# The low parts of eleven weight tiles are subtracted on GpSimd where VectorE did it

## The chip, the cores and the metric

The kernel runs on one core of one Trainium2 chip. The metric is the device time of one execution in microseconds (us); of several runs the median is given. The profile comes from one further execution. Engines are named as in the profile: PE is TensorE, DVE is VectorE, ACT is ScalarE, POOL is GpSimd, SP is the queue that starts DMAs.

## The reference

Attention with rotary positions (4 batches, 8 heads, 576 positions, head size 64) feeds a channel layer with a gate, and that a mixer of tokens and channels. Cut to what is computed:

```
attn = softmax(scale * rotate(q) @ rotate(k).T) @ v         # B=4, H=8, S=576, D=64
x    = attn, heads side by side                             # B x 576 x 512
xk, xr = mu * x + (1 - mu) * x_prev                         # mu_k and mu_r
v    = relu(xk @ w_k)**2 @ w_v                              # 512 -> 1024 -> 512
x    = sigmoid(xr @ w_r) * v                                # the gate: w_r is 512 x 512
h    = relu(x.T @ w_tok1) @ w_tok2                          # the token layer: 576 -> 256 -> 576
u    = x + h.T
out  = u + relu(u @ w_ch1) @ w_ch2                          # the channel layer: 512 -> 1536 -> 512
```

The weights arrive as 64-bit floats. Every product is made of two parts of each operand: `x` is rounded to a high part, and `x - high` is its low part; a product is then high*high + high*low + low*high.

## The kernel before, in words

**Stages.** Attention runs from the start to about 400 us. The channel layer of the middle (called K in the program) works through eight chunks (four batches, two halves of 288 positions), partly beside attention and from 400 us alone. Then come the gate and the token layer, from 488 us, and the last channel layer, from 597 us.

**One K chunk** (`kvr_gen`, L763). Eight groups of 12 products make `kp` (L751 to L753). Of each group ACT makes `t` (relu, L821) and the high part of its square `k2` (L825, called k in the profile); POOL makes the square again as `q` (L827); DVE subtracts, which gives the low part of `k2` (L828 through the helper `tt`, L111). The second product, `vp`, takes all eight `k2`, four groups of 24 products. For one `k2`, L751 and L753 need the high part, and L752 the low part. There are two buffers of `t`, two of `q`, and eight of `k2`.

**Weights** (class `Conv`, L183). Each weight tile passes four stages, in steps that take two tiles a time: SP loads its words (L207); ACT makes a first copy `cv` (L215); DVE turns the 64-bit words into 32-bit floats in `cv` with three instructions (L222, L226, L228), of which the second and third read `words` and `cv`; ACT writes the high part into `parts` (L80), and an engine subtracts, which gives the low part:

```
elif j == 3:
    dst, f = weights.take(k), self.t.pop(i).bitcast(F32)
    copy("A", dst[:, 0], f)
    tt(self.low, dst[:, 1], f, dst[:, 0].bitcast(F32), ALU.subtract)
```

The parameter `low` names that engine: "P" is POOL, anything else DVE. There are three `cv` buffers, so the ACT copy of the third tile on waits until the low part of a tile is subtracted. `conv0`, beside the start of attention, prepares the tiles of K, with "P". `conv1` (L995) prepares the four tiles of `w_r` (512 columns), five of `w_tok1` (256), two of `w_tok2` (576), and two of the last layer, which go another way (L246). It runs beside the last two K chunks, 433 to 475 us: the driver loop (L1050 to L1060) makes a step of `conv1` after every 45 products' worth of K.

**What sets the order.** The program names operations with priorities; a scheduler with a timing model of its own then fixes each engine's instruction order when the kernel is built. On the chip every engine takes its instructions strictly in that order, and waits on semaphores for what other engines owe it.

Of the kernel before, what the change touches and what calls it, by code (L numbers as in the profile page):

```python
# [16 lines left out]
B, H, S, D = 4, 8, 576, 64  # L17
# [14 lines left out]
HELD, LATE, EARLY = 5, 2, 2  # L32
# [39 lines left out]
def body(tc, kin, qin, vw, tabs, ident, mu, w_k, w_v, w_r, w_t1, w_t2, w_c1, w_c2, out):  # L72
# [41 lines left out]
    with ctx:  # L114
# [11 lines left out]
        P = {}  # L126
# [36 lines left out]
        def w3(w):  # L163
            return w.rearrange("(k p) f -> p k f", p=128)
# [516 lines left out]
        after = {}  # L681
# [191 lines left out]
        for j in range(2):  # L873
            for k in range(2):
# [3 lines left out]
        cv = Conv(lambda: P["xs"].tile([128, 2 * HS], I32, tag="xs", name="cv"),  # L878
                  wk + wv, "conv0", "rope", "P", lambda: acc_p.tile([128, 512], I32, tag="acc", name="cvp"))
# [32 lines left out]
        kv = Stream(kvr_gen([("K", b, c) for b in range(B) for c in range(2)], ready))  # L912
# [61 lines left out]
        def top(nm, bufs, st=mw):  # L974
            return st.enter_context(tc.tile_pool(name=nm, bufs=bufs, side="right"))

        cv_p = top("cv", 3)
        wr = Weights(top("wr", 1), [w3(w_r)[:, k] for k in range(KD)], [128, 2, DM])
        t1 = Weights(top("t1", 1), [w_t1[:, t] for t in range(5)], [128, 2, DTOK])
        t2 = Weights(top("t2", 1), [w_t2[:, m] for m in range(2)], [128, 2, S])  # L980
# [4 lines left out]
        def c2_part(a, b):  # L985
            w = Weights(top(f"c2{a}", 1), [w3(w_c2)[:, k] for k in range(a, b)], [128, 2, DM], raw_p, (rows2, a))
            c2_at.update({k: (w, k - a) for k in range(a, b)})
            return w
# [3 lines left out]
        def cv_t():  # L992
            return cv_p.tile([128, S], I32, tag="cv", name="cv")

        cv = Conv(cv_t, [wr, t1, t2, c2_part(0, EARLY)], "conv1", low="D", after="kv", then="out")  # L995
        def gate_gen(b):

            y = y_p[b].tile([128, KD, S], F32, tag="y", name="y")
# [73 lines left out]
        cv, cv3 = Conv(cv_t, [c1_w[0], c2_part(EARLY, HALF)], "conv2", low="D", after="gate"), Conv(cv_t, [c1_w[1], c2_b], "conv3", low="D", after="hs")  # L1072
# [234 lines left out]
```

## Time and profile before

| | |
|---|---|
| median of three runs | 901.6 us (901.35 to 908.77) |
| the profiled execution | 902.66 us, its span 900.8 us |
| mean granted PE clock | 0.988 of full |
| busy: PE, DVE, ACT, POOL | 839.5, 634.8, 515.3, 475.6 us |

The profile page gives sums over the span. The change touches only the stretch in which `conv1` runs, so the rows below come mostly from the timeline (instructions of one engine in order of time) and from the table of busy times by stretch, for 430 to 490 us. On the timeline a duration runs from an instruction's start to its end, and instructions of one engine overlap a little; how long each one holds its engine up is read from one start to the next.

### The profile page before, as it was taken

The numbers are of one execution on the slowest core, as the hardware profiler recorded it, in microseconds if no ns is written. First come the engines' busy times: TensorE is split into PE (matmuls) and PEld (weight loads), VectorE is DVE, ScalarE is ACT, GpSimd is POOL, SyncE is SP. The second block draws the span as 40 slices with busy tenths as digits, with TensorE's granted clock in tenths as the row PEclk, the third lists the DMA queues.
The fourth block names the chain that finished last, engine by engine and source line by source line (L and its number), as shares of the span: only waits on it lengthen the run. The fifth ranks groups of instructions, "written<-read, shape, count | busy, mean of one in ns | idle before, by whom it ended". The sixth has DMA issues, their size and how long they took to land.

```text
span 900.8 us, 18846 instructions
## 1 busy us (share of the span) xinstructions
PE 839.5 (93%) x7027; PEld 723.7 (80%) x7027; DVE 634.8 (70%) x1468; ACT 515.3 (57%) x1155; POOL 475.6 (53%) x506
## 2 busy tenths in 40 slices
PE   8899869898888899999999999999999999999998
PEld 5788757786776778799999989988878888888876
DVE  5889888887798788841793699956798355446332
ACT  4799678777777778863565656444556322223221
POOL 5999978988697666356344754311222222222221
PEclk9999979999999999999999999999999999999999
DMA  8786399999999979899332231201230000001000
GB/s 238 259 296 211 102 198 180 203 214 183 204 203 187 193 135 161 155 174 372 120 115 79 89 129 47 77 1 38 76 114 5 1 23 32 27 28 53 2 27 27
DMA packets 168651, 112.07 MB, mean 124 GB/s; under 512 B 132720, under 2 KB 148208, under 8 KB 168048
## 3 DMA queue, kind: packets, MB, share of 16 engines
q1 hardware_dynamic: 168560, 110.87, 49.6%
q8 instruction: 55, 0.90, 0.4%
q14 instruction: 36, 0.29, 0.1%
HBM read 60.90 MB, written 14.16 MB: 83 GB/s over the span
## 4 chain that ended last, share of the span: by engine, by line
PE 56%; DVE 17%; POOL 7%; ACT 7%; issue 6%; DMA 6%; SPq 1%; DVEq 0%; ACTq 0%; POOLq 0%
PE co L751 5%; PE c1p L751 5%; PE c1p L752 5%; PE c1p L753 5%; PE co L752 5%; PE co L753 5%; PE S L459 4%; DVE p L518 3%; PE pv L623 2%; DVE nm L477 2%; PE vp L751 2%; PE kp L751 2%; PE vp L752 2%; PE vp L753 2%; POOL rk L111 2%
## 5 line engine op out<-in xcount | busy, mean ns | idle before, releaser
L111 POOL TENSOR_TENSOR hs<-ht,hs 128x288 f16<-128x288 f32 x96 | 73.3, 764 | 229.6 <-DVE ht L1186 115.5
L1182 ACT ACTIVATE hs<-c1p,top 128x288 f16<-128x288 f32 x96 | 47.7, 497 | 161.7 <-PE c1p L753 161.7
L477 DVE TENSOR_REDUCE nm<-S 128x1 f32<-128x576 f32 x144 | 104.2, 748 | 16.1 <-PE S L459 15.1
L752 PE MATMUL c1p<-uhl,parts 128*128 128x288 f16 x384 | 109.8, 286 | 0.0
L753 PE MATMUL c1p<-uhl,parts 128*128 128x288 f16 x384 | 109.8, 286 | 0.0
L751 PE MATMUL c1p<-uhl,parts 128*128 128x288 f16 x384 | 109.6, 286 | 0.0
L752 PE MATMUL co<-hs,parts 128*128 128x288 f16 x384 | 108.7, 286 | 0.0
L753 PE MATMUL co<-hs,parts 128*128 128x288 f16 x384 | 108.7, 286 | 0.0
L751 PE MATMUL co<-hs,parts 128*128 128x288 f16 x384 | 105.1, 286 | 0.3 <-ACT hs L1182 0.3
L751 PEld LDWEIGHTS <-parts 128*128 128x128 f16 x768 | 75.0, 98 | 19.3 <-issue 0.5
L459 PE MATMUL S<-kq 64*128 64x288 f32 (+1 forms) x696 | 75.2, 317 | 16.2 <-ACT es L493 6.0
L751 PE MATMUL kp<-xs,parts 128*128 128x288 f32 x256 | 80.1, 316 | 11.0 <-ACT t L821 9.5
L752 PEld LDWEIGHTS <-parts 128*128 128x128 f16 x768 | 75.1, 98 | 18.8
L753 PEld LDWEIGHTS <-parts 128*128 128x128 f16 x768 | 75.2, 98 | 18.6
L1186 DVE TENSOR_SCALAR ht<-c1p,top 128x288 f32<-128x288 f32 x60 | 30.9, 515 | 77.6 <-ACT hs L1182 76.5
L111 POOL TENSOR_TENSOR q<-t 128x288 f32<-128x288 f32 x64 | 53.2, 835 | 59.2 <-ACT t L821 55.1
L459 PEld LDWEIGHTS S<-kq 64*128 64x128 f32 (+1 forms) x696 | 58.9, 191 | 30.2 <-ACT es L493 11.6
L751 PE MATMUL vp<-k,parts 128*128 128x288 f32 x256 | 77.2, 306 | 3.1 <-ACT vt L846 2.2
L518 DVE SCALAR_TENSOR_TENSOR p<-es,rc,p 128x576 f16<-128x576 f32 x60 | 68.0, 1137 | 13.8 <-ACT p L82 13.8
L752 PE MATMUL vp<-k,parts 128*128 128x288 f32 x256 | 76.7, 302 | 0.9 <-DVE k L111 0.9
L752 PE MATMUL kp<-xs,parts 128*128 128x288 f32 x256 | 76.6, 300 | 0.0
L753 PE MATMUL kp<-xs,parts 128*128 128x288 f32 x256 | 76.2, 298 | 0.0
(162 smaller groups left out, 2466.7 us busy)
## 6 DMA issues: line engine op xcount, KB each, us to landing
rq<-in_qin_dram SPq DMA_DIRECT2D x30, 320.0 KB, 4.0
rk<-in_kin_dram SPq DMA_DIRECT2D x30, 288.0 KB, 3.8
words<-in_w_c_dram SPq DMA_DIRECT2D x12, 512.0 KB, 3.8
words<-in_w_c_dram SPq DMA_DIRECT2D x16, 384.0 KB, 3.2
vr<-in_vw_dram SPq DMA_DIRECT2D x16, 320.0 KB, 3.4
xd<-xT SPq DMA_DIRECT2D x16, 288.5 KB, 2.8
xT<-xd SPq DMA_DIRECT2D x4, 1154.0 KB, 6.6
vd<-vt SPq DMA_DIRECT2D x32, 144.0 KB, 2.1
```

The source lines that it names most:

```text
L111: return (pool if e == "P" else dve).tensor_tensor(o, a, b, op=op)
L459: o = pe.matmul(S_t[j][:, h, 0:HS], lhsT=a[l, 128 * m:128 * m + 128], rhs=b[l, h * HS:(h + 1) * HS], start=(n == 0), stop=(n == 2))
L477: last["max"] = dve.tensor_reduce(out=nm, in_=S_t[j][:, :, 0:HS], op=ALU.max, axis=AX.XY, negate=True)
L518: o = last["lo"] = dve.scalar_tensor_tensor(out=t[:, 1], in0=e_t.pop(j), scalar=sum_t[j], in1=t[:, 0], op0=ALU.mult, op1=ALU.subtract)
L623: pe.matmul(p[l, 0:n], lhsT=v[:, a, l], rhs=ts[x][:, c, :], start=(i == 0), stop=(i == len(prods) - 1))
L751: pe.matmul(p, lhsT=wh, rhs=t[:, 0], start=first, stop=False)
L752: pe.matmul(p, lhsT=wh, rhs=t[:, 1], start=False, stop=False)
L753: pe.matmul(p, lhsT=wl, rhs=t[:, 0], start=False, stop=last)
L1182: last["hs"] = act.activation(out=h[:, 0], in_=p[:, 0:HS], func=AF.Relu, scale=g)
L1186: dve.tensor_scalar(out=f, in0=p[:, 0:HS], scalar1=g, scalar2=0.0, op0=ALU.mult, op1=ALU.max)
```

## The change

`conv1` gets "P" where it had "D":

```diff
-        cv = Conv(cv_t, [wr, t1, t2, c2_part(0, EARLY)], "conv1", low="D", after="kv", then="out")
+        cv = Conv(cv_t, [wr, t1, t2, c2_part(0, EARLY)], "conv1", low="P", after="kv", then="out")
```

Eleven subtractions go from DVE to POOL: four of 512 columns, five of 256, two of 576. The two tiles of the last layer go through L246 on DVE, as before. The scheduler makes its orders anew; they differ from before only in the stretch of the last two K chunks.

POOL's order in the chunk of batch 3, first half (`q` and `parts` with their numbers: `q_7085` is the square of the fourth `k2`, `q_7185` of the last; `parts_7207` is the last tile of `w_r`, `parts_7210` the first of `w_tok1`). Three subtractions of 512 columns stand further ahead in the same way.

```order
 L111 TENSOR_TENSOR q_7085<-t_7078 128x288
+L111 TENSOR_TENSOR parts_7207<-cv_7026,parts_7207 128x512
 L111 TENSOR_TENSOR q_7105<-t_7098 128x288
+L111 TENSOR_TENSOR parts_7210<-cv_7028,parts_7210 128x256
 L111 TENSOR_TENSOR q_7145<-t_7138 128x288
+L111 TENSOR_TENSOR parts_7294<-cv_7123,parts_7294 128x256
 L111 TENSOR_TENSOR q_7165<-t_7158 128x288
+L84 TENSOR_SCALAR a_7287<-xT_5620,om_s_74 128x288
+L111 TENSOR_TENSOR parts_7297<-cv_7125,parts_7297 128x256
 L111 TENSOR_TENSOR q_7185<-t_7178 128x288
-L84 TENSOR_SCALAR a_7287<-xT_5620,om_s_74 128x288
 L84 TENSOR_SCALAR a_7342<-xT_5620,om_s_74 128x288
```

Ahead of the last square, `q_7185`, POOL now has seven subtractions: four of 512 columns and three of 256.

DVE's order around the last `k2` of that chunk (`k2_7183`), before:

```order
L222 TENSOR_SCALAR cv_7125<-cv_7125 128x256
L738 SCALAR_TENSOR_TENSOR f_7254<-xT_5620,mu_s_73,a_7252 128x288
L111 TENSOR_TENSOR parts_7210<-cv_7028,parts_7210 128x256
L111 TENSOR_TENSOR k2_7183<-q_7185,k2_7183 128x288
L111 TENSOR_TENSOR parts_7294<-cv_7123,parts_7294 128x256
L226 SCALAR_TENSOR_TENSOR cv_7125<-words_7032,cv_7125 128x256
L111 TENSOR_TENSOR xs_7256<-f_7254,xs_7256 128x288
L222 TENSOR_SCALAR cv_7219<-cv_7219 128x256
```

The same place with the change:

```order
L111 TENSOR_TENSOR k2_7163<-q_7165,k2_7163 128x288
L111 TENSOR_TENSOR xs_7256<-f_7254,xs_7256 128x288
L226 SCALAR_TENSOR_TENSOR cv_7219<-words_7127,cv_7219 128x256
L222 TENSOR_SCALAR cv_7221<-cv_7221 128x256
L738 SCALAR_TENSOR_TENSOR f_7289<-xT_5620,mu_s_73,a_7287 128x288
L228 SCALAR_TENSOR_TENSOR cv_7219<-words_7127,cv_7219 128x256
L226 SCALAR_TENSOR_TENSOR cv_7221<-words_7129,cv_7221 128x256
L111 TENSOR_TENSOR k2_7183<-q_7185,k2_7183 128x288
L111 TENSOR_TENSOR xs_7291<-f_7289,xs_7291 128x288
```

Five subtractions ahead of `k2_7183` are gone from DVE (four of 512 columns, one of 256). In their place nine instructions that stood behind it now stand ahead of it: L226 and L228 of `cv_7125`; L222, L226 and L228 of `cv_7219`; L222 and L226 of `cv_7221`; one `xs`; one `f`.

PE's order where it first needs the low part of that `k2` (L752), before:

```order
L751 MATMUL vp_7233<-k2_7163,parts_1744 128x288
L752 MATMUL vp_7233<-k2_7163,parts_1744 128x288
L753 MATMUL vp_7233<-k2_7163,parts_1744 128x288
L752 MATMUL vp_7174<-k2_7183,parts_1747 128x288
L753 MATMUL vp_7174<-k2_7183,parts_1747 128x288
L751 MATMUL vp_7233<-k2_7183,parts_1747 128x288
```

With the change:

```order
L752 MATMUL vp_7268<-k2_7143,parts_1737 128x288
L753 MATMUL vp_7268<-k2_7143,parts_1737 128x288
L752 MATMUL vp_7174<-k2_7183,parts_1747 128x288
L753 MATMUL vp_7174<-k2_7183,parts_1747 128x288
L752 MATMUL vp_7233<-k2_7183,parts_1747 128x288
L753 MATMUL vp_7233<-k2_7183,parts_1747 128x288
L751 MATMUL vp_7268<-k2_7163,parts_1744 128x288
```

The first use of that low part stands 19 products later in PE's order, behind products of a third `vp` group. PE has the same number of products. On SP one load of `xT` (L1001) stands two stores earlier.

## Rows read from the trace of the kernel before

**Rows 1.** The page's first part: busy us, share of the span, instructions.

```profile
PE 839.5 (93%) x7027; PEld 723.7 (80%) x7027; DVE 634.8 (70%) x1468; ACT 515.3 (57%) x1155; POOL 475.6 (53%) x506
```

**Rows 2.** Table by stretch: us; busy PE, PEld, DVE, ACT, POOL; granted clock; DMA.

```profile
438.00:454.00 16.00, 15.85 (x120) 15.62 (x120) 16.00 (x31) 11.11 (x29) 7.46 (x9) 1.00 0.15 48
454.00:469.00 15.00, 15.00 (x116) 15.00 (x115) 14.28 (x32) 9.82 (x23) 5.56 (x3) 1.00 0.34 120
469.00:488.00 19.00, 18.17 (x136) 17.69 (x134) 10.47 (x19) 10.28 (x25) 8.91 (x12) 1.00 0.30 97
```

**Rows 3.** Timeline, PE: start, duration us, instruction, [idle before it, releaser].

```profile
448.16 0.29 PE L751 MATMUL vp<-k,parts 128*128 128x288 f32 x1
...
452.70 0.40 PE L752 MATMUL vp<-k,parts 128*128 128x288 f32 x1 [0.15 <-DVE k L111]
...
454.26 0.30 PE L752 MATMUL vp<-k,parts 128*128 128x288 f32 x1
...
477.02 0.41 PE L752 MATMUL vp<-k,parts 128*128 128x288 f32 x1 [0.75 <-DVE k L111]
...
595.87 0.41 PE L935 MATMUL trp<-idn,y 128*64 128x128 f32 x2 [1.53 <-DVE ytk L111]
```

**Rows 4.** Timeline, DVE, same columns.

```profile
441.80 0.92 DVE L111 TENSOR_TENSOR k<-q,k 128x288 fp32r<-128x288 f32 x1
...
443.24 0.68 DVE L111 TENSOR_TENSOR parts<-cv,parts 128x512 fp32r<-128x512 f32 x1
443.85 0.68 DVE L226 SCALAR_TENSOR_TENSOR cv<-words,cv 128x512 int32<-128x512 int32 x1
...
452.20 0.45 DVE L111 TENSOR_TENSOR k<-q,k 128x288 fp32r<-128x288 f32 x1
452.57 0.28 DVE L222 TENSOR_SCALAR cv<-cv 128x256 int32<-128x256 int32 x1
452.77 0.51 DVE L738 SCALAR_TENSOR_TENSOR f<-xT,mu_s,a 128x288 f32<-128x288 f32 x1
453.20 0.41 DVE L111 TENSOR_TENSOR parts<-cv,parts 128x256 fp32r<-128x256 f32 x1
453.53 0.45 DVE L111 TENSOR_TENSOR k<-q,k 128x288 fp32r<-128x288 f32 x1
...
463.53 0.75 DVE L111 TENSOR_TENSOR parts<-cv,parts 128x576 fp32r<-128x576 f32 x1
464.20 0.74 DVE L228 SCALAR_TENSOR_TENSOR cv<-words,cv 128x576 int32<-128x576 int32 x1
```

**Rows 5.** Timeline, POOL, same columns, in the same stretch.

```profile
428.90 0.51 POOL L84 TENSOR_SCALAR a<-xT,om_s 128x288 f32<-128x288 f32 x1 [0.41 <-DVE f L738]
...
441.69 0.72 POOL L111 TENSOR_TENSOR q<-t 128x288 f32<-128x288 f32 x1 [1.06 <-DVE k L111]
...
456.51 2.33 POOL L84 TENSOR_SCALAR a<-xT,om_s 128x288 f32<-128x288 f32 x1 [2.24 <-DVE f L738]
466.04 3.80 POOL L111 TENSOR_TENSOR q<-t 128x288 f32<-128x288 f32 x2 [7.20 <-ACT t L821]
470.30 1.37 POOL L111 TENSOR_TENSOR q<-t 128x288 f32<-128x288 f32 x2 [0.46 <-DVE k L111]
```

**Rows 6.** View of tile `parts` on POOL: duration ns min/median/max, first and last start.

```profile
L111 POOL TENSOR_TENSOR parts<-cv,parts x16: 1267/1284/1910, 30.7 to 95.9; 128x512 fp32r<-128x512 f32 x16
```

**Rows 7.** Timeline, POOL, beside attention: two other widths with two inputs.

```profile
82.76 1.43 POOL L111 TENSOR_TENSOR rk<-rk 128x576 f32<-128x576 f32 x1
...
93.65 0.80 POOL L111 TENSOR_TENSOR xs<-f,xs 128x288 fp32r<-128x288 f32 x1
```

**Rows 8.** Views of tiles `rp`, `t1p`, `t2p`: first users of the moved tiles, columns as in rows 6.

```profile
L751 PE MATMUL rp<-xs,parts x128: 291/295/400, 488.5 to 589.3; 128*128 128x288 f32 x128
L948 PE MATMUL t1p<-ytk,parts x64: 277/281/386, 504.9 to 631.7; 128*128 128x256 f32 x64
L963 PE MATMUL t2p<-parts,h x64: 290/296/403, 513.0 to 643.5; 128*128 128x288 f32 x64
```

## Prediction

> **What bounds the kernel now.** I read the page's busy shares first: PE is busy 839.5 us of the span, far ahead of any other engine [rows 1]. So an edit to DVE and POOL counts only where it makes PE wait, or ends a wait of PE. The eleven subtractions lie between 433 and 475 us, so the table by stretch came next. From 438 to 454 us PE is busy 15.85 of 16.00 us and DVE all 16.00; from 454 to 469 us PE never pauses, and DVE works 14.28 of 15.00; from 469 to 488 us PE loses 0.83 us [rows 2]. POOL has most of its time free there (7.46 busy of 16.00). Two engines are full, then, and the question is which one holds the other. PE's timeline answers: it waits for the low part of a `k2` from DVE twice, 0.15 us at 452.70 and 0.75 us at 477.02 [rows 3]. PE bounds the stretch, and DVE follows so closely behind that it has no slack left. That is the appeal of the edit, and its limit: if every wait of PE on those low parts went away, 0.9 us would be won, since PE's number of products stays. The granted clock is 1.00 in all three stretches [rows 2], the upper level, 2.4 GHz.
>
> **What the change takes from DVE.** From start to start, a subtraction of 512 columns costs DVE 0.61 us (443.24 to 443.85), one of 256 costs 0.33 (453.20 to 453.53), one of 576 costs 0.67 (463.53 to 464.20) [rows 4]. All eleven: 4 x 0.61 + 5 x 0.33 + 2 x 0.67 = 5.4 us.
>
> **What it gives POOL.** The same subtraction of 512 columns, made by POOL for `conv0`, has a median of 1.28 us [rows 6]. 576 columns with two inputs take 1.43, and 288 take 0.80 [rows 7]. Between 288 and 512 that is 0.00214 us a column, so 256 columns come to 0.73. All eleven: 4 x 1.28 + 5 x 0.73 + 2 x 1.43 = 11.6 us. By free time alone POOL could take this.
>
> **What the two engines do to each other.** The price that decides is not in a column of busy time. A `k` on DVE takes 0.45 us at 452.20, while POOL is idle. The `k` at 441.80 takes 0.92 [rows 4], and POOL had begun a `q` at 441.69 that took 0.72 [rows 5]. DVE lost 0.47 us to one POOL instruction of 0.72, all but 0.25 of it. The reverse is seen as well: POOL's `a` takes 0.51 us at 428.90 and 2.33 at 456.51, where DVE runs without a gap, and a pair of `q` takes 1.37 at 470.30 but 3.80 at 466.04 [rows 5]. Instructions of DVE and POOL that read SBUF mostly exclude each other in this stretch. I therefore price each new POOL subtraction at its duration less 0.25 us of DVE's time: 1.03, 0.48 and 1.18 us for 512, 256 and 576 columns. The trace shows no subtraction of this form beside these DVE instructions, so that is an estimate from the nearest pair. The lowest price is nothing (full overlap; less is excluded, since DVE's saving is counted apart), the highest the whole POOL duration. I take the middle one because its row has the same two engines, the same stretch and two-input instructions on DVE.
>
> The Trainium skill has a rule on this, which speaks against the change: SBUF — State Buffer, section "SBUF: two separate sides", says that VectorE and GpSimd share a pair of ports as an exclusive lock, held for a whole instruction, against VectorE instructions with two SBUF inputs or in a two-port mode. The row at 441.80 agrees in direction, but shows 0.47 us lost of 0.72. By the rule the full POOL durations would be charged; carried through the two steps below, it gives +6.1 us in place of +3.4, a result inside the forecast's range.
>
> **First place: the chunk of batch 3, first half.** In the new order POOL makes seven subtractions ahead of the last `q`, which cost DVE 4 x 1.03 + 3 x 0.48 = 5.6 us. DVE no longer makes the five that stood ahead of the last `k2`: 4 x 0.61 + 0.33 = 2.8 back. But the scheduler filled the gap, pulling nine instructions ahead of it: five conversions of 256 columns (L226, L228, taken at the same 0.33), two shifts (0.20: 452.57 to 452.77), one `xs` (as a `k`, 0.37: 452.20 to 452.57) and one `f` (0.43: 452.77 to 453.20) [rows 4]. Together 1.65 + 0.4 + 0.8 = 2.9 us. So the last `k2` comes 5.6 - 2.8 + 2.9 = 5.7 us later: it starts at 453.53 + 5.7 = 459.2 and ends at 459.7. PE first wanted it at 454.26 [rows 3]: the 44th product after 448.16, by PE's order. From 448.16 to there, less the wait, a product takes 0.13 us, so the 19 products that now stand ahead give 2.5 us, and PE wants it at 456.8. PE waits about 2.9 us in this chunk, shared over several `k2`, against 0.15: **+2.8 us**.
>
> **Second place: the second half.** Four subtractions remain (two of 256, two of 576): 2 x 0.48 + 2 x 1.18 = 3.3 us of hold. DVE saves the remaining six of its own, 4 x 0.33 + 2 x 0.67 = 2.7 us, and the 2.9 us already done earlier. So the `k2` of this half come 5.7 + 3.3 - 2.7 - 2.9 = 3.4 us later, and PE itself is 2.8 us late: 0.6 us on top of the wait at 477.02. **+0.6 us.**
>
> **At nothing.** The moved low parts themselves are not awaited: `w_r` is first used at 488.5 us, `w_tok1` at 504.9, `w_tok2` at 513.0 [rows 8], while the last tile of `w_r` is subtracted ahead of the first of `w_tok1` at 453.20, and the first of `w_tok2` at 463.53 [rows 4]; a delay of 6 us leaves over 25. If that cover were gone, the gate would start late by the whole delay. ACT's first copies of the weights now wait for POOL to free a `cv` buffer, and behind them on ACT stand the `t` and the high parts of `k2`; this is part of the same chain (`q` can't start before `t`), and the two `t` and two `q` buffers carry it. The load of `xT` that passes two stores on SP is wanted after the gate of the first batch began, far off. PE's new waits are pieces of about a microsecond; at 595.87 it waited 1.53 us [rows 3], so I charge no clock. What is late next is the gate, which needs `xs` from DVE, ACT and POOL; these follow the same shift.
>
> **Sum.** The profiled execution took 902.66 us (span 900.8 and 1.9 around it): 902.7 + 2.8 + 0.6 = 906.1. The median of the runs shown, 901.6, lies 1.1 lower, so I expect 901.6 + 3.4 = **905.0 us**.
>
> **Rivals.**
> - *A free ride.* POOL reads while DVE works on something that does not clash, DVE keeps its 5.4 us, and the low parts of `k2` come in time. For it: POOL is more than half idle, and the order on PE gives 2.5 us of grace. Against it: the stretched rows of both engines. Both waits go at best, 901.6 - 0.9 = 900.7 us; with a little clash, up to 902.5. Chance 0.28.
> - *POOL starved (slower).* DVE runs gapless there, and a POOL instruction that loses waits long: `a` lost 1.8 us (2.33 against 0.51), a `q` of the pair 1.2. POOL is in order, so every `q` stands behind a starved subtraction. If each of the seven loses 1.8 us, POOL owes 4 x 1.28 + 3 x 0.73 = 7.3 us of work and 7 x 1.8 = 12.6 of starving, 19.9 us, less the 8.5 it has free from 438 to 454 and the 2.5 of PE's order, 8.9 us of waiting in the first chunk alone: 901.6 + 8.9 = 910.5, more with the second. It decides from about 1.8 us a piece; below 1.3 its price is lost in the forecast's. Against it: while POOL makes DVE wait for `q`, DVE has gaps, and POOL gets its turn. Chance 0.07.
> - *No move at all.* Excluded by the built order: eleven instructions fewer on DVE, eleven more on POOL.
>
> **How the numbers follow.** Forecast, +1.5 to +6.5 us: 0.62. Free ride: 0.28. Starved: 0.07. The remaining 0.03 is for what I do not see, such as a better phase in the gate stage. From the forecast I keep the upper bound: full holds with no help from PE's order or DVE's relief, 7.3 + 2 x 0.73 + 2 x 1.43 = 11.6 less 2.7 won back in the second half, 8.9, or 910.5, which is where starving begins. The range that leaves out no more than 2 in 10 goes from the free ride's best, 900.7, to 908.5. A measurement of this kernel can tell about 1%, 9 us, from no change. Faster by that: 0.02, as nothing shown offers 9 us. Slower by that: the starved case where it decides, 0.06. Within: 0.92.
>
> **What would show it.** In the changed trace: eleven `parts` on POOL at 433 to 475 us, of 1.3 us and more for 512 columns; DVE's `k`, `cv` rows at 0.9 us and over beside them; PE's waits for DVE `k` in the `vp` of the first of the two chunks adding up to some 3 us, and 1 to 1.5 in the second; the first `rp` at about 492 us where it was 488.5; after that the same times shifted. If the `cv` rows of DVE keep 0.33 and 0.61 while POOL subtracts, the clash is wrong and the free ride holds. If `q` on POOL stands idle for ACT's `t` instead, the chain through the `cv` buffers is the cause. Waits of PE of over 8 us would mean starving.

## The result, and the profile after

The changed kernel takes 912.8 us (median of six runs, 910.95 to 913.64), the kernel before 904.9 in the six runs beside it (901.35 to 908.97). The ratio is 1.0092, with a 95% interval from 1.0063 to 1.0122: slower, and beyond the upper end of the range, 908.5. The profiled execution took 912.41 us, 9.75 more than that of before. By these medians the change costs 7.9 us, by the interval of the ratio 5.7 to 11.0. Of the 7.8 us between the forecast of 905.0 and the result, 3.3 lie in the base (901.6, the median of three runs, where six have 904.9), and 4.5 in the change itself.

The page's first part for the changed kernel, as in [rows 1], shows where the work went, and not the time:

```profile
PE 843.2 (93%) x7027; PEld 724.9 (80%) x7027; DVE 641.7 (70%) x1457; ACT 515.5 (57%) x1155; POOL 488.5 (54%) x517
```

DVE has eleven instructions fewer and is busy 6.9 us longer. The time itself lies in one stretch: from the first `kp` of batch 3's first half to the first product of the gate (`rp`) there were 53.0 us before (435.44 to 488.47) and there are 63.4 now (435.07 to 498.47). What comes before and after it is as long as it was, within 0.4 us. All times within a kernel are those of its one profiled execution. The table by stretch, same columns as [rows 2]:

```profile
438.00:454.00 16.00, 13.67 (x100) 13.04 (x99) 15.83 (x21) 9.85 (x25) 13.42 (x13) 1.00 0.16 48
454.00:469.00 15.00, 13.52 (x98) 12.78 (x96) 12.47 (x24) 6.20 (x16) 5.37 (x8) 1.00 0.29 99
469.00:488.00 19.00, 14.90 (x101) 14.20 (x102) 15.52 (x23) 10.88 (x26) 10.86 (x11) 0.96 0.32 89
```

In the first row DVE is as busy as before with 21 instructions in place of 31, and PE loses 2.3 us; in the third the granted clock is below 1.00. PE's timeline shows its waits in the stretch, as in [rows 3]:

```profile
450.57 0.40 PE L752 MATMUL vp<-k,parts 128*128 128x288 f32 x1 [1.11 <-DVE k L111]
...
453.12 0.40 PE L752 MATMUL vp<-k,parts 128*128 128x288 f32 x1 [1.22 <-DVE k L111]
...
455.98 0.40 PE L752 MATMUL vp<-k,parts 128*128 128x288 f32 x1 [0.61 <-DVE k L111]
...
458.04 0.40 PE L752 MATMUL vp<-k,parts 128*128 128x288 f32 x1 [0.45 <-DVE k L111]
...
470.76 0.40 PE L751 MATMUL kp<-xs,parts 128*128 128x288 f32 x1 [2.18 <-ACT vt L846]
...
482.67 0.40 PE L752 MATMUL vp<-k,parts 128*128 128x288 f32 x1 [0.40 <-DVE k L111]
...
484.56 0.53 PE L751 MATMUL vp<-k,parts 128*128 128x288 f32 x2 [1.36 <-ACT k L825]
...
485.93 0.40 PE L752 MATMUL vp<-k,parts 128*128 128x288 f32 x1 [0.58 <-DVE k L111]
```

Four waits for low parts in the first half (3.4 us), one for ACT's `vt` at the start of the second half, three in its `vp`, one of them for ACT. Right behind the last three the granted clock falls to its lower level, 1.2 GHz, from 486.4 to 489.8 us; the table by stretch, cut finely:

```profile
486.70:487.60 0.90, 0.90 (x5) 0.90 (x5) 0.90 (x2) 0.00 (x0) 0.68 (x1) 0.50 0.00 0
...
490.10:491.00 0.90, 0.90 (x9) 0.90 (x8) 0.00 (x0) 0.82 (x2) 0.81 (x1) 1.00 0.00 0
```

PE looks fully busy in both rows, but has 5 products under way in 0.90 us where it has 9 at the upper level: from one start to the next a product takes 0.24 us there, and 0.13 otherwise. Counted from one product's start to the next, less the usual 0.13 us, the stretch loses: 4.0 us in the first half (0.3 before), 2.3 at the `kp` (0), 2.8 in the second half (0.9), 0.7 at the `rp` (0.7), and 2.4 more than before in many small steps. Of those, 14 products at the lower clock make 1.5 us, and one step of 0.24 right behind each wait makes the other 0.9. Together 3.7 + 2.3 + 1.9 + 1.5 + 0.9 = 10.3 of the 10.4 us.

Where DVE's time went is in the groups by line and form, 430 to 490 us (count, busy us, mean ns). Of the kernel before:

```profile
L228 DVE SCALAR_TENSOR_TENSOR cv<-words,cv 128x512 int32<-128x512 int32 x6 | 5.0, 838 | 0.0
...
L226 DVE SCALAR_TENSOR_TENSOR cv<-words,cv 128x256 int32<-128x256 int32 x5 | 2.5, 506 | 0.0
```

Of the changed kernel:

```profile
L228 DVE SCALAR_TENSOR_TENSOR cv<-words,cv 128x512 int32<-128x512 int32 x6 | 7.7, 1280 | 0.2
L111 POOL TENSOR_TENSOR parts<-cv,parts 128x512 fp32r<-128x512 f32 x4 | 6.4, 1610 | 7.3 <-ACT parts L80 7.3
...
L226 DVE SCALAR_TENSOR_TENSOR cv<-words,cv 128x256 int32<-128x256 int32 x5 | 3.7, 739 | 0.0
```

The merges of the weights' words (L226, L228), which the change does not move, got longer beside POOL's subtractions: the two groups shown by half, all those of 512 and 256 columns together from 14.2 to 20.0 us. POOL's subtractions of 512 columns take 1610 ns in place of the 1284 of [rows 6]. On the timelines the pairs can be seen; the last row of DVE is the last `k2` of the first half, which before stood at 453.53 in [rows 4]:

```profile
437.97 1.79 DVE L228 SCALAR_TENSOR_TENSOR cv<-words,cv 128x512 int32<-128x512 int32 x1
...
441.83 1.55 DVE L111 TENSOR_TENSOR k<-q,k 128x288 fp32r<-128x288 f32 x1
...
459.92 0.68 DVE L111 TENSOR_TENSOR k<-q,k 128x288 fp32r<-128x288 f32 x1
```

POOL:

```profile
437.71 1.50 POOL L111 TENSOR_TENSOR parts<-cv,parts 128x512 fp32r<-128x512 f32 x1 [7.05 <-ACT parts L80]
...
441.32 1.75 POOL L111 TENSOR_TENSOR parts<-cv,parts 128x512 fp32r<-128x512 f32 x1
```

The first two of DVE began just behind these subtractions and ended 0.3 to 0.6 us after them.

### The profile page after: what moved, and what is told of

It is laid out like the page before. It is cut to its first block, busy times and chain, and to the rows that moved or that the text cites. A ratio compares the mean times of both kernels' runs of the same rounds, so it can differ in the third digit from the quotient of the medians.

```text
span 910.6 us, 18849 instructions
## 1 busy us (share of the span) xinstructions
PE 843.2 (93%) x7027; PEld 724.9 (80%) x7027; DVE 641.7 (70%) x1457; ACT 515.5 (57%) x1155; POOL 488.5 (54%) x517
## 4 chain that ended last, share of the span: by engine, by line
PE 52%; DVE 17%; POOL 10%; DMA 6%; ACT 6%; issue 6%; SPq 2%; DVEq 0%; ACTq 0%; POOLq 0%
PE co L751 5%; PE c1p L751 5%; PE c1p L752 5%; PE c1p L753 5%; PE co L752 5%; PE co L753 5%; DVE p L518 4%; DMA rk<-in_kin_dram 3%; POOL rk L111 3%; POOL rq L111 3%; DVE nm L477 3%; PE S L459 2%; PE kp L751 2%; PE vp L751 2%; PE vp L752 2%
## 5 line engine op out<-in xcount | busy, mean ns | idle before, releaser
L477 DVE TENSOR_REDUCE nm<-S 128x1 f32<-128x576 f32 x144 | 104.3, 749 | 18.1 <-PE S L459 17.6
L752 PE MATMUL c1p<-uhl,parts 128*128 128x288 f16 x384 | 109.8, 286 | 0.0
L752 PE MATMUL co<-hs,parts 128*128 128x288 f16 x384 | 108.7, 286 | 0.0
L752 PEld LDWEIGHTS <-parts 128*128 128x128 f16 x768 | 75.1, 98 | 18.9
L751 PE MATMUL vp<-k,parts 128*128 128x288 f32 x256 | 77.2, 308 | 6.0 <-ACT vt L846 3.6
L752 PE MATMUL vp<-k,parts 128*128 128x288 f32 x256 | 77.7, 305 | 4.6 <-DVE k L111 4.4
L752 PE MATMUL kp<-xs,parts 128*128 128x288 f32 x256 | 77.1, 302 | 2.7 <-POOL xs L111 2.7
L753 PE MATMUL vp<-k,parts 128*128 128x288 f32 x256 | 76.1, 298 | 0.0
```

What stands on the lines that cost most here:

```text
L477: last["max"] = dve.tensor_reduce(out=nm, in_=S_t[j][:, :, 0:HS], op=ALU.max, axis=AX.XY, negate=True)
L751: pe.matmul(p, lhsT=wh, rhs=t[:, 0], start=first, stop=False)
L752: pe.matmul(p, lhsT=wh, rhs=t[:, 1], start=False, stop=False)
L753: pe.matmul(p, lhsT=wl, rhs=t[:, 0], start=False, stop=last)
```

## The experiments

My theory after the result had two causes: DVE instructions that read two operands from SBUF take turns with POOL's subtractions, and the load of `xT` on SP holds up the stores behind it. Rivals: the turns alone make all of it, and the load is only where it shows; or the new order on DVE alone makes `k2` late. In the table, "stretch" runs from the first `kp` of batch 3's first half to the first `rp`; the waits are PE's, by the profile's column, in the first half's `vp` / at the `kp` / in the second half's `vp`; the last column counts falls of the granted clock to the lower level in the stretch. The ratios of e1 to e4 go by one set of runs of before (903.4), those of e5 to e7 by another (904.0), those of e8 and e9 by a third (903.2).

| kernel | median us | ratio to before, 95% | stretch us | waits us | clock falls |
|---|---|---|---|---|---|
| before | | 1 | 53.0 | 0.2 / 0 / 0.8 | 0 |
| changed | 912.8 | 1.0092 [1.0063, 1.0122] | 63.4 | 3.4 / 2.2 / 2.3 | 1 |
| e1 changed, load behind stores | 912.6 | 1.0094 [1.0058, 1.0130] | 60.8 | 2.4 / 0 / 2.3 | 2 |
| e2 before, load ahead of stores | 906.6 | 1.0032 [1.0007, 1.0057] | 56.6 | 0.2 / 2.9 / 0 | 1 |
| e3 before, `w_r` alone on POOL | 906.5 | 1.0040 [1.0014, 1.0067] | 55.8 | 2.0 / 0 / 0 | 1 |
| e4 before, `w_tok1`, `w_tok2` on POOL | 907.6 | 1.0048 [1.0014, 1.0083] | 57.2 | 0.9 / 0 / 1.6 | 1 |
| e5 before, PSUM, load behind | 905.2 | 1.0006 [0.9981, 1.0032] | 51.5 | 0 / 0 / 0 | 0 |
| e6 changed, PSUM, load behind | 903.4 | 0.9979 [0.9952, 1.0006] | 51.5 | 0 / 0 / 0 | 0 |
| e7 before, `w_tok2` alone on POOL | 906.3 | 1.0020 [0.9994, 1.0046] | 55.7 | 0.1 / 0 / 1.9 | 1 |
| e8 changed, PSUM | 901.7 | 0.9989 [0.9961, 1.0017] | 51.5 | 0 / 0 / 0 | 0 |
| e9 before, PSUM | 901.0 | 0.9998 [0.9964, 1.0031] | 51.5 | 0 / 0 / 0 | 0 |

**e1 and e2: the load on SP, taken back and made alone.** In the new order the load of batch 1's `xT` (L1001) stands ahead of the four stores of `vt` (L847); before, two stores went first. The load must wait for DVE's last lerp (`f`, L738), which reads the buffer that it fills. SP's wait for it, 440 to 480 us, in the changed kernel (what is waited for: us in total, times, longest), where it was 1.3 us before:

```profile
SPq L1001 <- DVE f L738: 21.6, 1, 21.6
```

Nobody waits for the load. But the stores behind it free ACT's two `vt` buffers, and ACT pays; behind its second row here stand the copies and the `t` of the second half. The changed kernel, ACT:

```profile
463.08 0.39 ACT L846 ACTIVATE vt<-vp 128x288 f32<-128x288 f32 x1
...
470.30 0.81 ACT L846 ACTIVATE vt<-vp 128x288 f32<-128x288 f32 x2 [4.09 <-DMA vd<-vt]
```

SP, and the load's size and time from issue to landing:

```profile
462.30 0.32 SPq L1001 DMA_DIRECT2D xT<-xd  x1
463.49 8.04 SPq L847 DMA_DIRECT2D vd<-vt  x4
...
xT<-xd SPq DMA_DIRECT2D x1, 1154.0 KB, 6.0
```

SP's own wait held no store here: the load was gone at 462.62, the first `vt` was done at 463.47, and its store was issued at 463.49. It is the load's transfer, under way just ahead, behind which the store lands: 6.7 us after its issue, where the stores of e1, with no load ahead of them, take 1.7 to 2.5. DVE's lateness is what puts that transfer so late.

e1 edits the changed kernel:

```diff
-    sp.dma_start(vd[b][c][:, m], vt)
+    last[f"vd{b}{c}"] = sp.dma_start(vd[b][c][:, m], vt)
...
-    sp.dma_start(x, xd[b])
+    behind(sp.dma_start(x, xd[b]), "vd30" if b == 1 else "none")
```

> The changed kernel with one SP instruction moved: the load of xT for the second gate batch stands behind the four vt stores of the chunk of batch 3, first half, not ahead of them; the order on PE, DVE, ACT and POOL stays as in the changed kernel. From the first kp product of that chunk to the first rp product the kernel before takes 53.0 us, the changed one 63.4. Theory A (two causes: DVE and POOL exclude each other, and the load that waits for DVE's last f holds up the stores, the vt buffers and ACT): ACT no longer waits 4.1 us for vd<-vt, PE no longer waits 2.2 us before a kp product, PE's four waits for k in the first chunk stay at 3.4 us; the stretch comes to 57 to 59 us, and the time to 0.4 to 0.6% over before. Theory B (the exclusion of DVE and POOL alone makes all of it, the blocked store is only where it shows): the stretch stays at 62 to 64 us and the time at 0.8 to 1.1% over before.

The wait at the `kp` went, and the stretch got 2.6 us shorter; 60.8 lies between the two ranges, so both missed. The time, 0.94% over before, lies in theory B's range; against the changed kernel it moved by less than its interval can tell. The first half's waits stayed, and so did those of the second half, which is therefore not late because of SP.

e2 puts the stores behind the load in the kernel before:

```diff
-    sp.dma_start(vd[b][c][:, m], vt)
+    last[f"vd{b}{c}{m}"] = sp.dma_start(vd[b][c][:, m], vt)
...
-    sp.dma_start(x, xd[b])
+    p = sp.dma_start(x, xd[b]); [order(last[f"vd30{m}"], p) for m in range(2) if b == 1]
```

> The kernel before (all subtractions on DVE) with the load of xT for the second gate batch put ahead of the four vt stores on SP, as the change put it; the scheduler then also reorders a few rows of the second chunk. Theory A: SP waits for DVE's last f of that chunk (near 459 us), the stores land only behind the load's 1.15 MB, ACT waits 2 to 5 us for a vt buffer and PE 1 to 4 us, the stretch grows from 53.0 to 54.5 to 57 us, the time by 0.15 to 0.45%. Theory B: the stretch stays within 1 us of 53.0.

PE's timeline shows the one new wait, and the clock fell behind it (0.50 from 472 to 474 us):

```profile
471.31 0.61 PE L751 MATMUL kp<-xs,parts 128*128 128x288 f32 x1 [2.92 <-ACT vt L846]
```

The theory's range held. So this order costs 3.6 us with all subtractions on DVE. Here SP held the first store as well, from 461.2 to 463.6 us, and it landed 7.2 us after its issue.

**e3 and e4: the change in two parts.** Both are the kernel before with some of the subtractions on POOL; e3:

```diff
-    tt(self.low, dst[:, 1], f, dst[:, 0].bitcast(F32), ALU.subtract)
+    tt("P" if self.name == "conv1" and weights is wr else self.low, dst[:, 1], f, dst[:, 0].bitcast(F32), ALU.subtract)
```

> The kernel before with only the four subtractions of w_r (512 columns) on POOL; the SP order is that of before, the five tiles of w_tok1 and two of w_tok2 stay on DVE. Exclusion of DVE and POOL (theory A's first cause): DVE rows beside the four POOL rows stretch by 0.5 to 1 us each, PE's waits for k in the first chunk add up to 2 to 3.5 us (0.15 before), little after; stretch 55 to 57 us, time 0.2 to 0.4% over before. Rival (the new DVE order alone, nine instructions pulled ahead of the last k, costs the first chunk's waits, no exclusion): this kernel has less pulled ahead, so waits under 1 us and a stretch of 53 to 54 us.

e4 has `weights is not wr` in the same place.

> The kernel before with only the seven subtractions of w_tok1 and w_tok2 (256 and 576 columns) on POOL, all of which stand behind the last q of the first chunk; SP order as before. Theory A: they lie where POOL has nothing to do and no k waits on DVE, so the first chunk's waits stay near 0.15 us, the second chunk's between 0.5 and 1.5 us (0.75 before); stretch 52.5 to 54 us, time within 0.2% of before. Rival (each POOL subtraction costs its DVE time wherever it stands): 2 x 0.5 + 3 x 0.5 + 2 x 1.2 less 3.0 saved, about +2 us.

e3's waits lie in the first half alone, as expected (1.11 and 0.93 us, for DVE's `k`), and are more than the rival's 1 us. e4's stretch grew by 4.1 us, which is more than either of its ranges: its waits lie in both halves. The two parts add to 2.8 + 4.1 = 6.9 us, near the 7.8 that e1 has over before.

**e7: the two tiles of 576 columns alone**, as e3 with `weights is t2`.

> The kernel before with only the two 576-column subtractions of the second token layer on GpSimd. Theory A (they hold conversion buffers longer and stretch VectorE in the second half-chunk, where TensorE waits for k and t): first half-chunk as before (waits below 0.5 us), second half-chunk's waits 1.5 to 3 us against 0.9, stretch 54 to 57 us. Rival (the second half-chunk is late only because the first was): stretch within 0.7 us of before's 53.0 us, no wait above 1 us but the two that stand there before.

The theory's ranges held: the first half is as before, and the second has one new wait. Its way can be followed through three timelines. DVE:

```profile
464.25 1.88 DVE L228 SCALAR_TENSOR_TENSOR cv<-words,cv 128x576 int32<-128x576 int32 x1
...
468.69 1.15 DVE L228 SCALAR_TENSOR_TENSOR cv<-words,cv 128x512 int32<-128x512 int32 x1
```

ACT:

```profile
474.96 1.33 ACT L82 ACTIVATE parts<-cv,rows 128x512 f16<-128x512 f32 x2 [3.67 <-DVE rows L138]
476.20 0.69 ACT L821 ACTIVATE t<-kp 128x288 f32<-128x288 f32 x2
```

PE:

```profile
476.64 0.40 PE L751 MATMUL vp<-k,parts 128*128 128x288 f32 x1 [1.88 <-ACT t L821]
```

A merge of `w_tok2` takes 1.88 us beside a POOL subtraction, those of the last layer's two tiles behind it come late, ACT waits for their row maxima, and its `t` stand behind that in its order. The second half thus has a cause of its own, worth 2.6 us with the fall of the clock behind it.

**m1 and m2: the clash by itself.** Barriers part the stretches; the core of m1 is

```
two(24, 256, m)        # DVE: L226's form, both inputs in SBUF
two(24, 256, mp)       # the same, one input in PSUM
one(24, 256)           # DVE: L222's form
sub(8, 512)            # POOL: the subtraction
...
two(48, 256, m); sub(12, 512)     # both engines at once
two(48, 256, mp); sub(12, 512)
one(72, 256); sub(12, 512)
```

> Leaves the whole computation of the reference out (it writes zeros) and measures the disputed cost by itself: stretches with only VectorE working, only GpSimd working, and both. VectorE: 256-column L228-like merges with both inputs in SBUF, the same with one input in PSUM, and shifts; GpSimd: subtractions of 512, 256 and 576 columns of fp32. Theory A (the two engines share something for an instruction with two SBUF inputs; that is what the chunk of batch 3 shows): beside a stream of GpSimd subtractions the two-SBUF merge takes 1.5 times or more of its time alone (411 ns in the kernel), and the subtraction more than 1.3 us against about 1.03 us alone; the merge with one input in PSUM keeps its time within 10%, and so does the shift. Theory B (the longer durations in the changed kernel are waits inside the chain, not contention): all three keep their times within 10%. Theory C (a lock for a whole instruction on any VectorE work): all three stretch alike.

Groups by line and form of m1, each from one stretch (8.1 to 16.2, 16.3 to 24.2, 29.6 to 39.5; both engines 57.2 to 74.0 and 86.0 to 100.9):

```profile
L62 DVE SCALAR_TENSOR_TENSOR cv<-words,m 128x256 int32<-128x256 int32 x24 | 8.1, 420 | 0.0
...
L62 DVE SCALAR_TENSOR_TENSOR cv<-words,mp 128x256 int32<-128x256 int32 x24 | 8.0, 418 | 0.0
...
L58 POOL TENSOR_TENSOR lo<-f,hi 128x512 fp32r<-128x512 f32 x8 | 9.8, 1263 | 0.0
...
L62 DVE SCALAR_TENSOR_TENSOR cv<-words,m 128x256 int32<-128x256 int32 x14 | 17.6, 1327 | 0.0
L58 POOL TENSOR_TENSOR lo<-f,hi 128x512 fp32r<-128x512 f32 x12 | 16.9, 1440 | 0.0
...
L62 DVE SCALAR_TENSOR_TENSOR cv<-words,mp 128x256 int32<-128x256 int32 x46 | 15.3, 411 | 0.0
L58 POOL TENSOR_TENSOR lo<-f,hi 128x512 fp32r<-128x512 f32 x12 | 14.9, 1281 | 0.0
```

With two operands in SBUF the engines alternate, about one merge for each subtraction (14 and 12 in the stretch). From start to start a merge alone takes 8.13 / 24 = 0.34 us, a subtraction alone 9.80 / 8 = 1.23, a pair of them 16.87 / 12 = 1.41: all but 0.16 us of the sum. With one operand in PSUM 46 merges ran beside the same twelve subtractions at their lone duration. Theory A held for the merges, B and C fell; the shifts did something else, told below. Alone the subtraction takes 1.26 us, and not the 1.03 of the expectation.

m2 does the same with other forms.

> Leaves the whole computation of the reference out (it writes zeros) and measures which VectorE instructions take turns with GpSimd's 512-column subtraction: fp32 sums of two SBUF tiles of 288 columns (the form of k), shifts from SBUF into PSUM, a mix of shift, shift into PSUM and merge with one PSUM operand, and 512-column merges of two SBUF tiles. Theory A (an instruction of VectorE that reads two SBUF operands, or runs at the shift's doubled rate out of and into SBUF, excludes GpSimd for its whole length; one that touches PSUM does not): sums beside GpSimd 1.2 us or more each, 512-column merges 1.6 us or more, shifts into PSUM as alone, and GpSimd's subtraction at 1.26 us beside them; in the mix GpSimd waits only in the plain shifts. Rival (only the bitwise merge is special): the sums keep their time alone.

Groups of m2: sums alone (8.7 to 17.5), sums beside POOL (29.1 to 46.3), shifts into PSUM beside POOL (55.1 to 69.7):

```profile
L80 DVE TENSOR_TENSOR k<-f,hi 128x288 fp32r<-128x288 f32 x24 | 8.9, 454 | 0.0
...
L80 DVE TENSOR_TENSOR k<-f,hi 128x288 fp32r<-128x288 f32 x13 | 17.7, 1430 | 0.0
L61 POOL TENSOR_TENSOR lo<-f,hi 128x512 fp32r<-128x512 f32 x12 | 17.3, 1472 | 0.0
...
L61 POOL TENSOR_TENSOR lo<-f,hi 128x512 fp32r<-128x512 f32 x12 | 14.7, 1264 | 0.0
L75 DVE TENSOR_SCALAR mp<-m 128x256 int32<-128x256 int32 x33 | 14.1, 428 | 1.1
```

The form of `k` takes turns as the merges do, so the bitwise operation is not special. The 512-column merges did not alternate at all, against my expectation: they kept their time, and POOL stood still. In the mix the expectation failed too: it was DVE's plain shift that waited (0.58 us, 0.30 alone), while a subtraction took 1.27 us from start to start, 1.23 alone.

**e5, e6, e8, e9: the clash taken out of the kernel.** The words between L222 and L228 go to a PSUM buffer for tiles of up to 512 columns, so that L226 and L228 read one operand from there:

```diff
-    m = self.room()[:, :w] if self.room else v
+    m = self.room()[:, :w] if self.room and w <= 512 else v
...
-    if self.room:
+    if self.room is not None:
...
-    "conv1", low="P", after="kv", then="out")
+    "conv1", low="P", after="kv", then="out", room=lambda: pv_p.tile([128, 512], I32, tag="pv", name="cvp"))
```

e8 is the changed kernel with this alone, e9 the kernel before with it (and "D"). e6 and e5 are the same two with e1's edit as well. The edit does a second thing: with `room` given, `step` takes its two tiles one after the other (the branch behind `if self.room`), so in all four kernels the conversions also stand in another order on DVE.

> The kernel before, with the intermediate words of the background conversion (tiles of up to 512 columns) written to a PSUM buffer in place of SBUF, so that VectorE's two merges read one operand from PSUM, and with the load of the next batch's inputs behind all four stores of the chunk. Low parts stay on VectorE. Theory A: the stretch from the first kp of the chunk to the first rp stays at 52 to 54 us (there is little GpSimd work beside VectorE here to clash with) and the time is that of before within 0.4%. Rival: the PSUM buffer is shared with the projections' outputs and adds a wait for it: stretch 55 us or more.

> The changed kernel with the same two edits: conversion's intermediate in PSUM for tiles of up to 512 columns, load behind the four stores. Theory A (first chunk's waits come from VectorE's merges being stretched beside GpSimd's subtractions): TensorE's waits in the first half-chunk fall from 4.0 to below 1 us, no stretch of granted clock at half follows them, the second half-chunk keeps about 1.5 to 2.5 us of its own (its 576-column tiles are not moved), stretch 54 to 58 us, kernel's ratio to before 1.001 to 1.005. Rival (the waits come from the order on VectorE alone, nine instructions ahead of the last k2): stretch stays at 60 to 62 us as with the load moved alone, ratio about 1.009.

> The changed kernel with the conversion's intermediate in PSUM (tiles of up to 512 columns) and nothing else: the load of the next batch's inputs stays ahead of the four stores on SP. Theory A (clash and SP order are two separate causes): TensorE's waits for k in both half-chunks are gone as in the run with both edits, one wait of 2 to 3 us at the kp of the second half-chunk remains (ScalarE's vt held by the stores behind the load), with one stretch of half clock behind it; stretch from first kp to first rp 54 to 57 us, ratio to before 1.001 to 1.004. Rival (the load's wait is only there because VectorE was late): no such wait, stretch 51 to 52.5 us.

> The kernel before with the conversion's intermediate in PSUM (tiles of up to 512 columns) and nothing else. Theory A (before had a little of the same clash, VectorE's merges against GpSimd's q): stretch 51 to 52.5 us against before's 53.0, ratio to before 0.996 to 1.000. Rival (the 1.5 us that the two earlier runs with PSUM gained came from the load's place): stretch 53 us.

A group of e8, 430 to 490 us (its stretch lies later, 441.9 to 493.4):

```profile
L228 DVE SCALAR_TENSOR_TENSOR cv<-words,cvp 128x512 int32<-128x512 int32 x6 | 4.1, 682 | 0.2
```

and its table by stretch:

```profile
438.00:454.00 16.00, 16.00 (x123) 16.00 (x122) 12.35 (x20) 11.93 (x28) 9.30 (x10) 1.00 0.27 85
454.00:469.00 15.00, 15.00 (x115) 15.00 (x114) 14.64 (x30) 9.13 (x24) 7.59 (x11) 1.00 0.30 100
469.00:488.00 19.00, 19.00 (x146) 19.00 (x145) 13.52 (x24) 12.44 (x30) 11.32 (x14) 1.00 0.33 97
```

L228 fell from 1280 ns to 682, PE does not pause in any row, the clock stays at 1.00, and the stretch fell from 63.4 to 51.5 us: all that the change cost, and 1.5 us that before loses too. e9, also at 51.5, lies in its theory's range: those 1.5 us do not come from the load's place. In e6 I expected 1.5 to 2.5 us of wait to remain in the second half, and in e5 a stretch of 52 us or more; both came out below. Why the 576-column tiles, which still merge in SBUF, cost nothing there is not shown; in e8 their merges keep 751 ns.

Because of the other order, these four can't by themselves exclude the rival that the new order on DVE makes `k2` late. From the first `kp` to the last `k2` of the first half DVE starts 34 instructions in the changed kernel and 28 in e6, in 24.8 and 17.2 us; by the start-to-start times of the kernel before (as in [rows 4]), the six are worth 1.7 of the 7.6 us. e3, which has none of this edit, settles it. By those same times DVE's instructions up to there come to 12.8 us in the kernel before and in the changed one, and to 11.7 in e3; they took 18.1, 24.8 and 21.7. With less to do than before, e3 is 3.6 us later: it is the duration of the instructions and not their order.

e8 also settles SP, and for the rival. The load stands ahead of all four stores there too, the first store lands 4.7 us after its issue, ACT waits for it, and PE does not. SP's timeline in e8, then ACT's:

```profile
461.48 0.32 SPq L1001 DMA_DIRECT2D xT<-xd  x1
463.07 7.23 SPq L847 DMA_DIRECT2D vd<-vt  x4
```

```profile
467.85 0.41 ACT L846 ACTIVATE vt<-vp 128x288 f32<-128x288 f32 x1 [2.46 <-DMA vd<-vt]
```

Counted from the first `kp` of the stretch, the load was issued after 19.6 us (from 441.88), against 27.2 in the changed kernel (462.30 from 435.07) and 24.0 in e2 (463.16 from 439.18). The place on SP is harmless where DVE's lerps are in time, and passes DVE's lateness on to ACT and PE where they are not; in e2 they are late enough with the subtractions still on DVE.

None of e5, e6, e8 and e9 is shown to beat the kernel before: their stretches are 1.5 us shorter, and the intervals of the ratios hold 1. All four beat the changed kernel, by intervals that do not meet its own.

## Why the prediction was wrong

**Right: what bounds the stretch, and the price of the clash.** I charged 1.03 us of DVE's time for a subtraction of 512 columns, from one row of 0.47 lost of 0.72 [rows 4, 5]. m1 gives 1.41 - 0.34 = 1.07 beside merges. The rule of the Trainium skill (SBUF — State Buffer, "SBUF: two separate sides") is nearly what m1 shows: an exclusive lock would hold the whole instruction, and 0.16 us of a pair of 1.57 overlaps. The "`cv` rows at 0.9 us and over" came, and the free ride is excluded.

**Right in kind, a little small: the first place.** The last `k2` was to start at 459.2 us and started at 459.92; PE was to lose 2.8 us more and lost 3.7.

**Mis-sized: the second place.** I said +0.6 us and it was +1.9. I followed the low parts of `k2` from POOL to DVE. The larger wait, 1.36 us, is for ACT, on which the scaled copy of the last layer's tiles (L82) stands ahead of `t`:

```profile
482.24 1.33 ACT L82 ACTIVATE parts<-cv,rows 128x512 f16<-128x512 f32 x2 [3.08 <-DVE rows L138]
```

ACT waited 3.08 us there for DVE, against 1.36 before. e7 shows the mechanism with two subtractions alone. I had put ACT at nothing, as "part of the same chain"; it is another chain, through another tile.

**Failed: "the load of `xT` that passes two stores on SP is wanted after the gate of the first batch began, far off".** I asked when the load is wanted, and not what follows it on SP. The stores behind it land late and free ACT's `vt` late, and that was 2.3 us at the `kp`. e2 has the same wait from the order alone (2.92 us), e1 is without it, and e8 shows that it also takes a late lerp on DVE.

**Failed: "I charge no clock".** I leant on one wait of 1.53 us with no fall behind it [rows 3]. The falls came at or just behind a single wait of 1.9 us (e7) and of 2.9 (e2), and at the second of two of 1.11 and 0.93 within 2.3 us of each other (e3). Here one fall cost 1.5 us, and the long step behind each wait, which I had not counted either, 0.9.

The sum: 0.9 + 1.3 + 2.3 + 1.5 + 0.9 = 6.9 us over the 3.4 that I forecast, as the stretch has it. The range ended at 908.5, 0.4 above the forecast's +6.5 and with no term of its own; the result lies beyond the bound of 910.5 too, which had neither the stores nor the clock in it. The starving rival gave about the time that came, but not its mechanism: POOL's `q` took 892 ns on average in the stretch against 970 before, and the first half's waits were 3.4 us, not 8.9.

## What to carry to other kernels

Before moving work from VectorE to GpSimd, look at what VectorE will run beside it. In the forms measured here, instructions that read an operand from PSUM or write there ran beside GpSimd at their lone durations; with two SBUF operands the engines took turns, and a subtraction held VectorE for nearly its whole length (1.07 of 1.23 us in m1). Long runs of shifts within SBUF, and of 512-column merges, made GpSimd stand still instead. When an engine gets late, go through every in-order queue behind it (here SP's load, and ScalarE's copy for another layer) and ask what stands behind the instruction that waits, not when its own result is wanted. Where TensorE gains waits of a microsecond or two, put a fall of its clock into the range; here it cost 1.5 us, as much as a wait.

## What the runs showed of the hardware beside this

GpSimd can be shut out for a whole run of VectorE instructions. In m1 POOL's one-column instruction was asked for just behind the first of 72 plain shifts within SBUF (L67), and ended with the last of them; the timeline:

```profile
101.71 14.63 DVE L67 TENSOR_SCALAR cv<-m 128x256 int32<-128x256 int32 x72
101.87 14.52 POOL L53 TENSOR_TENSOR bar<-bar 128x1 f32<-128x1 f32 x1 [0.96 <-DVE bar L50]
```

DVE lost nothing (294 ns each, 296 alone). In m2 fourteen merges of 512 columns did the same for 8.40 us:

```profile
101.08 8.51 DVE L65 SCALAR_TENSOR_TENSOR cv<-words,m 128x512 int32<-128x512 int32 x14
101.24 8.40 POOL L56 TENSOR_TENSOR bar<-bar 128x1 f32<-128x1 f32 x1 [7.92 <-DVE bar L53]
```

while merges of 256 columns and sums of 288 let the first POOL instruction through after 0.3 us and then alternated. What decides between the two stays open: the same fourteen merges, in the stretch just ahead, let such an instruction through after 0.57 us.

In each of the six kernels in which PE's waits grew (the changed one, e1 to e4, e7), the clock fell to the lower level, during a wait or up to 0.7 us behind one, and in the stretch of the others it did not. Not every wait did it: in the changed kernel those of 1.11 and 1.22 us and the one of 2.18 had no fall behind them, nor had the 1.53 us of [rows 3] in any kernel.
